# Block-sparse attention feeding a gated MLP: the four dense attention units stand first instead of last in each pair of batches

## The chip, the cores and the metric

One core of a Trainium2 chip runs the whole kernel. The metric is the device time of one execution in microseconds (us). The time before is the median of three runs, 783.1 us (782.36 to 784.8).

## The reference

Block-sparse attention over 4 batches, 8 heads, 768 positions of 64 values; a block is 32 positions, so there are 24 blocks. Its output, laid out as 3072 tokens of 512 values, goes through two matrices with a gate between them.

```python
scores = scale * np.matmul(q, k.transpose(0, 1, 3, 2))
mask = np.abs(blk_i - blk_j) <= window                                   # own block and its neighbours
mask = mask | (blk_i == 0) | (blk_j == 0) | (blk_i == n_blocks - 1) | (blk_j == n_blocks - 1)
...                                                                      # and 3 sampled blocks for each query block
attn = softmax(np.where(mask, scores, -1e9)); out = attn @ v
h = x @ w_in;  g = h * (1.0 / (1.0 + np.exp(-1.702 * h)));  return g @ w_out
```

Query blocks 0 and 23 see all 24 key blocks; every other query block sees at most eight.

## The kernel before

**Units.** Attention is cut into 48 units of 64 query positions (two blocks) with all heads. A *sparse unit* is two neighbouring blocks of 1 to 22 in one batch; it is one *item* of work. A *dense unit* is blocks 23 and 0 of one batch; it is four items (`i` picks two head pairs, `half` picks 384 of the 768 keys). A unit gives 64 columns of x for the MLP.

**An item** is: `scores` (PE; then on VectorE, DVE, the masked minimum, L283, called *least* here, and on ScalarE, ACT, the exponentials, L290), `transposes` (PE L306, then two ACT copies to `pt`, L310), `values` (PE L331 sparse, L339 dense). At the end of a unit come `factors` and `normalise` (small DVE work; for a dense unit seven small operations with a short ACT exponential between them, and three multiplies and adds, L373 and L377, instead of one), then `turn` (two PE transposes, the ACT cast `xhi`, the DVE difference `xlo`).

**Loads.** A pair of batches shares one K and one V load for each pair of blocks (`load_k`, `load_v`): contiguous pieces from SyncE's queue (SP), the sampled K blocks by SP and in the first stage also by GpSimd (POOL), the gathered V rows by POOL (L216). A dense unit has its own loads: 1.5 MB of K (L183), two V halves of 768 KB, and q. K and V have rings of two buffers each, so `loads` issues an entry when the one two before it is used up.

**The MLP** takes the tokens in 6 chunks of 512 (8 units). One chunk has 16 *ticks* (`tick`): 12 matmuls of `up`, the gate, 12 matmuls of `down`. The weights come as 64-bit words and are made into pairs of fp32r tiles during the first stage and the first 16 ticks by a generator (`weights`). For each tile it has four places where it yields: fetch and shift (L446); the low part of the tile before (L427, *last*); a DVE merge (L452) with ACT's `Abs` of the next raw tile (L422); a second DVE merge (L456) with ACT's cast (L459). It stops at the fourth `wout` tile until the first `down` is done, since `wout` has a ring of three.

**Order of the work.** Every engine works off its own list in program order. `first` runs the items of units 0 to 8 before any tick (the *first stage*), one item behind another: scores of item n, then turn of n-2, transposes of n-1, exponentials of n, values of n-1. It advances the weight generator four times per item (two before, two after), and has four spare PE transposes per item (L693). Later units are spread over the ticks by `plan`: chunk c's attention is done while the MLP works on chunk c-1. Before the change units 0 to 8 are all sparse, and dense units are 22, 23, 46 and 47.

Of the kernel before, what the change touches and what calls it, by code (L numbers as in the profile page):

```python
# [43 lines left out]
class Kernel:  # L44
# [4 lines left out]
    def __init__(self, ctx, tc, q, qd, kb, kT, v, vd, sb, w_in, w_out, out):  # L49
# [25 lines left out]
        def entry(of, **more):  # L75
            of.append({"n": len(of), "scores": 0, "values": 0, **more})
            return of[-1]
# [5 lines left out]

        for b0 in range(0, B, 2):
            for u in range(NU):
                k, v = (entry(of, b=b0, u=u) for of in (self.kent, self.vent))
                for b in (b0, b0 + 1):
                    entry(self.units, b=b, u=u)
                    item(k, v, first=True, end=True)
            for b in (b0, b0 + 1):  # L90
                entry(self.units, b=b, u=None)
                k = entry(self.kent, b=b, u=None)
                for i in range(2):
                    v = entry(self.vent, b=b, u=None, i=i)
                    for half in range(2):
                        item(k, v, i=i, half=half, first=i + half == 0, end=i + half == 2)
# [80 lines left out]
    def load_k(self, e):  # L177
# [3 lines left out]
        if u is None:  # L181
            nc.sync.dma_start(out=self.qt[r][:, 0], in_=self.qd[:, b])
            nc.sync.dma_start(out=self.kg[r].rearrange("p n b c -> p (n b c)"), in_=self.kT[b])  # L183
            self.kmidof[r] = None
            return
# [34 lines left out]
    def loads(self):  # L220

        more = True
        while more:
# [141 lines left out]
    def normalise(self, g):  # L365
# [4 lines left out]
        if not self.sparse(g):  # L370
            out.append(self.work.tile([P, 384], F32, name="ex", bufs=4)[:, 0:2 * P])
# [150 lines left out]
    def down(self, m, part):  # L522
# [13 lines left out]
        if m == NC * NF - 1:  # L536
            order = order[-1:] + order[:-1]
# [130 lines left out]
    def first(self):  # L668

        items = self.items[:CU + 1]  # L670
        assert items[CU]["unit"]["n"] == CU
# [9 lines left out]
        for n, g in enumerate(items):  # L681
# [4 lines left out]
            if n > 1:  # L686
                weights(2)
                finish(self.turn(items[n - 2]))
            if n > 0:
                finish(self.transposes(items[n - 1]))  # L690

                for _ in range(4):
                    self.nc.tensor.matmul(self.psum("a", n - 1)[0][:, 3 * P:4 * P], self.ident, self.ident, start=True, stop=True)  # L693
# [4 lines left out]
            if n > 1:  # L698
                weights(2)
        finish(self.transposes(items[CU]))  # L700
        finish(self.turn(items[CU - 1]))
# [65 lines left out]
```

## Time and profile before

| | |
|---|---|
| runs | 783.1 us median of 3 (782.36 to 784.8) |
| profiled execution: span, first to last instruction | 782.1 us |
| PE busy | 743.4 us (95%) |
| DVE busy / ACT busy | 413.0 us (53%) / 382.6 us (49%) |
| HBM read / written | 116.47 MB / 10.49 MB |

What lies around the span of the profiled execution isn't shown by itself; the median of the runs is 1.0 us above that span. The page's 40 slices show PE filled from about 80 us on and with holes before, while the DMA engines are busiest in the first 80 us. Engines named PEld, SPq and ACTq are PE's weight loads and the queues of SyncE and ScalarE.

### The profile page before, as it was taken

How to read it: one execution, taken by the hardware profiler on the slowest of the kernel's cores; microseconds unless marked ns; L12 is line 12 of the kernel's file. 1: busy time of each engine (PE TensorE's matmuls, PEld its weight loads, DVE VectorE, ACT ScalarE, POOL GpSimd, SP SyncE). 2: the span in 40 equal slices, each digit the busy share in tenths (PEclk: the TensorE clock that was granted, in tenths of full speed). 3: DMA queues.
4: the chain of work that ended last, by engine and by line, in shares of the span. 5: the costliest groups of instructions: out<-in, count | busy, mean ns of one | idle time of the engine just before them, and what ended most of it. 6: DMA issues, size and time to landing. Idle time of an engine off the chain costs nothing.

```text
span 782.1 us, 19390 instructions
## 1 busy us (share of the span) xinstructions
PE 743.4 (95%) x7648; PEld 580.5 (74%) x7648; DVE 413.0 (53%) x1076; ACT 382.6 (49%) x950; POOL 56.2 (7%) x85
## 2 busy tenths in 40 slices
PE   2876999999999999999999999999999999999997
PEld 1655787777777777787787787877778777888885
DVE  4486689978545344455445445445555444443332
ACT  1566667766555454454544544444555444333232
POOL 5222001101000001000000000000000000000000
PEclk9899999999999999999999999999999999999999
DMA  8998787886644346663544564544574231141111
GB/s 264 288 332 282 271 258 233 293 269 190 210 167 149 95 150 195 180 192 116 163 129 123 155 183 127 153 128 137 165 247 156 81 107 30 41 108 41 54 41 55
DMA packets 61117, 128.22 MB, mean 164 GB/s; under 512 B 7569, under 2 KB 26514, under 8 KB 60514
## 3 DMA queue, kind: packets, MB, share of 16 engines
q1 hardware_dynamic: 46642, 80.11, 33.8%
q0 software_dynamic: 7232, 25.51, 9.9%
q10 hardware_dynamic: 7152, 21.37, 8.2%
q8 instruction: 60, 0.98, 0.5%
q14 instruction: 31, 0.25, 0.1%
HBM read 116.47 MB, written 10.49 MB: 162 GB/s over the span
## 4 chain that ended last, share of the span: by engine, by line
PE 79%; DMA 7%; DVE 6%; ACT 4%; issue 2%; SPq 1%; ACTq 0%; DVEq 0%
PE bank L491 11%; PE bank L544 10%; PE bank L493 10%; PE bank L545 10%; PE bank L540 10%; PE bank L492 10%; PE bank L306 5%; PE bank L331 4%; PE bank L260 4%; DMA raw<-in_moe_w_in_dram 3%; PE bank L339 2%; PE bank L272 2%; DMA kg<-in_kb_dram 1%; DMA ws<-a 1%; DVE a L452 1%
## 5 line engine op out<-in xcount | busy, mean ns | idle before, releaser
L491 PE MATMUL bank<-xhi,win 128*128 128x512 f32 x384 | 158.7, 413 | 1.6 <-DVE g L506 1.3
L290 ACT ACTIVATE ex<-bank,nm 128x256 f32<-128x256 f32 (+1 forms) x208 | 99.5, 491 | 117.4 <-DVE nm L283 115.6
L506 DVE SCALAR_TENSOR_TENSOR g<-g,bank 128x512 f32<-128x512 f32 x83 | 57.1, 687 | 183.9 <-ACT g L499 183.9
L544 PE MATMUL bank<-wout,ghi 128*128 128x512 f32 x384 | 154.0, 401 | 0.0
L545 PE MATMUL bank<-wout,ghi 128*128 128x512 f32 x384 | 151.7, 395 | 0.0
L493 PE MATMUL bank<-xhi,win 128*128 128x512 f32 x384 | 151.1, 394 | 0.0
L492 PE MATMUL bank<-xlo,win 128*128 128x512 f32 x384 | 150.0, 391 | 0.0
L499 ACT ACTIVATE g<-bank 128x512 f32<-128x512 f32 x96 | 57.5, 599 | 148.3 <-PE bank L493 147.7
L540 PE MATMUL bank<-wout,glo 128*128 128x512 f32 x384 | 107.8, 394 | 0.0
L480 DVE TENSOR_TENSOR wout<-wst,wout 128x512 fp32r<-128x512 f32 x80 | 55.4, 692 | 79.6 <-ACT wout L479 78.6
L511 ACT CAST ghi<-g 128x512 fp32r<-128x512 f32 x96 | 59.7, 622 | 56.2 <-DVE g L506 56.2
L491 PEld LDWEIGHTS bank<-xhi,win 128*128 128x128 f32 x384 | 72.1, 188 | 19.7 <-DVE g L506 2.0
L540 PEld LDWEIGHTS bank<-wout,glo 128*128 128x128 f32 x384 | 72.5, 189 | 17.2
L493 PEld LDWEIGHTS bank<-xhi,win 128*128 128x128 f32 x384 | 72.1, 188 | 16.4
L545 PEld LDWEIGHTS bank<-wout,ghi 128*128 128x128 f32 x384 | 72.6, 189 | 15.6
L544 PEld LDWEIGHTS bank<-wout,ghi 128*128 128x128 f32 x384 | 72.2, 188 | 16.0
L283 DVE CUSTOM_DVE_ANT_1 bank<-bank,bias 128x256 f32<-128x256 f32 x176 | 73.8, 440 | 18.6 <-PE bank L260 15.6
L492 PEld LDWEIGHTS bank<-xlo,win 128*128 128x128 f32 x384 | 72.4, 188 | 13.0
L216 POOL DMA_INDIRECT vown<-in_v_dram,vidx x44 | 42.8, 973 | 501.5 <-PE bank L331 390.0
L310 ACT COPY pt<-bank 128x512 f32<-128x512 f32 (+1 forms) x120 | 61.1, 564 | 19.4 <-PE bank L306 19.1
L260 PE MATMUL bank<-kg,qt 64*32 64x256 f32 x1408 | 53.0, 405 | 16.2 <-DMA vmid<-in_v_dram 10.7
L519 DVE TENSOR_TENSOR glo<-g,ghi 128x512 fp32r<-128x512 f32 x96 | 65.7, 684 | 1.6 <-ACT ghi L511 1.6
(77 smaller groups left out, 815.3 us busy)
## 6 DMA issues: line engine op xcount, KB each, us to landing
wst<-ws SPq DMA_DIRECT2D x80, 256.0 KB, 2.7
kg<-in_kb_dram SPq DMA_DIRECT2D x136, 128.0 KB, 3.8
kg<-in_kb_dram SPq DMA_DIRECT2D x22, 384.0 KB, 5.1
raw<-in_moe_w_in_dram ACTq DMA_DIRECT2D x16, 512.0 KB, 5.1
raw<-in_moe_w_out_dram ACTq DMA_DIRECT2D x16, 512.0 KB, 4.6
kg<-in_kT_dram SPq DMA_DIRECT2D x4, 1536.0 KB, 7.5
vown<-in_vd_dram SPq DMA_DIRECT2D x8, 768.0 KB, 5.1
qt<-in_q_dram SPq DMA_DIRECT2D x22, 256.0 KB, 3.0
```

Source lines behind the costliest of these rows:

```text
L260: nc.tensor.matmul(sps[h][BLK * c:BLK * (c + 1), n * i:n * (i + 1)].rearrange("p (n s) -> p n s", s=BLK), self.qt[r][rows, bi, UT * pair + ...
L283: nc.vector.tensor_tensor_reduce(out=at, in0=at, in1=bias, scale=-SCALE, scalar=3.0e38, op0=ALU.add, op1=ALU.min, accum_out=un["nm"][:, ha ...
L290: nc.scalar.activation(out=ex, in_=sps[h][:, n * k:n * (k + 1)], func=AF.Exp, bias=un["nm"][:, half, c:c + 1], scale=-1.0, accum_out=un["r ...
L310: copies.append(lambda pt=pt, ps=ps, m=m: nc.scalar.copy(out=pt[:, 0:m], in_=ps[:, 0:m]))
L491: nc.tensor.matmul(h, wih[:, k], hi[:, k], start=(k == 0), stop=False)
L492: nc.tensor.matmul(h, wih[:, k], lo[:, k], start=False, stop=False)
L493: nc.tensor.matmul(h, wil[:, k], hi[:, k], start=False, stop=(k == NCT - 1))
L511: self.nc.scalar.copy(out=ghi, in_=self.g[m][0])
L519: self.nc.vector.tensor_tensor(out=glo, in0=g, in1=ghi.bitcast(F32), op=ALU.subtract)
L540: nc.tensor.matmul(o[n], glo[:, tk[n]], woh, start=False, stop=last)
L544: nc.tensor.matmul(o[n], ghi[:, tk[n]], woh, start=(f == 0), stop=False)
L545: nc.tensor.matmul(o[n], ghi[:, tk[n]], wol, start=False, stop=False)
```

## The change

The list of units begins with the four dense units (one per batch), then come the sparse ones in the order they had. Chunk 0 is now 4 dense and 4 sparse units, the other chunks are 8 sparse units each. `first` still takes units 0 to 8; these are now 21 items (16 dense, 5 sparse) instead of 9. In a dense item the generator advances once, not four times, and after a dense item there are no spare transposes. The K load of a dense unit is cut in two halves, and the first loads are K of unit 0 and both its V halves. One scratch tile of `normalise` comes from another pool, and the last `down` has its plain order again.

```diff
+        for b in range(B):
+            entry(self.units, b=b, u=None)
+            k = entry(self.kent, b=b, u=None)
+            for i in range(2):
+                v = entry(self.vent, b=b, u=None, i=i)
+                for half in range(2):
+                    item(k, v, i=i, half=half, first=i + half == 0, end=i + half == 2)
         for b0 in range(0, B, 2):
             for u in range(NU):
...
-            for b in (b0, b0 + 1):
-                entry(self.units, b=b, u=None)
...
-            nc.sync.dma_start(out=self.kg[r].rearrange("p n b c -> p (n b c)"), in_=self.kT[b])
+            kg, n = self.kg[r].rearrange("p n b c -> p (n b c)"), NPAIR // 2 * S
+            for i in range(2):
+                nc.sync.dma_start(out=kg[:, n * i:n * (i + 1)], in_=self.kT[b, :, n * i:n * (i + 1)])
...
+        if not self.knext:
+            self.load_k(self.kent[0])
+            for e in self.vent[:RING]:
+                self.load_v(e)
+            self.knext, self.vnext = 1, RING
...
-            out.append(self.work.tile([P, 384], F32, name="ex", bufs=4)[:, 0:2 * P])
+            out.append(self.work.tile([P, 4, P], F32, name="pt").rearrange("p a b -> p (a b)")[:, 0:2 * P])
...
-        if m == NC * NF - 1:
-            order = order[-1:] + order[:-1]
...
-        items = self.items[:CU + 1]
-        assert items[CU]["unit"]["n"] == CU
+        items = [g for g in self.items if g["unit"]["n"] <= CU]
...
             if n > 1:
-                weights(2)
-                finish(self.turn(items[n - 2]))
+                weights(2 if self.sparse(g) else 1)
+                if items[n - 2]["end"]:
+                    finish(self.turn(items[n - 2]))
             if n > 0:
                 finish(self.transposes(items[n - 1]))
-
+            if n > 0 and self.sparse(items[n - 1]):
+
+                spare = self.psum("a", items[n - 1]["unit"]["n"])[0][:, 3 * P:4 * P]
                 for _ in range(4):
-                    self.nc.tensor.matmul(self.psum("a", n - 1)[0][:, 3 * P:4 * P], self.ident, self.ident, start=True, stop=True)
+                    self.nc.tensor.matmul(spare, self.ident, self.ident, start=True, stop=True)
...
-            if n > 1:
+            if n > 1 and self.sparse(g):
                 weights(2)
-        finish(self.transposes(items[CU]))
-        finish(self.turn(items[CU - 1]))
+        finish(self.transposes(items[-1]))
+        finish(self.turn(items[-2]))
```

**ACT, a sparse item in the middle of the first stage.** `raw` and `a` are tiles of the weight generator, `win` and `wout` the finished weights, `ws` their copy in memory, `bank_88` and `bank_92` hold the transposes of the item before. Before:

```order
L459 CAST wout_118<-a 128x512
L414 DMA raw<-in_moe_w_in_dram 128x1024
L433 DMA ws_70<-a 128x512
L422 ACTIVATE a<-raw 128x512
L391 CAST xhi_120<-bank_91 128x4x64
L310 COPY pt<-bank_88 128x512
L310 COPY pt<-bank_92 128x512
L290 ACTIVATE ex,rs<-bank_89,nm 128x256 x2
L290 ACTIVATE ex,rs<-bank_90,nm 128x256 x2
L459 CAST win_104<-a 128x512
```

Now, at the same place (an item between two sparse items):

```order
L440 DMA ws_70<-a 128x512
L429 ACTIVATE a<-raw 128x512
L466 CAST win_104<-a 128x512
L421 DMA raw<-in_moe_w_out_dram 128x1024
L398 CAST xhi_120<-bank_87 128x4x64
L317 COPY pt<-bank_88 128x512
L317 COPY pt<-bank_92 128x512
L297 ACTIVATE ex,rs<-bank_85,nm 128x256 x2
L297 ACTIVATE ex,rs<-bank_86,nm 128x256 x2
```

The generator stands two yields further on at this place, so its cast moved from behind the exponentials to a place ahead of the copies.

**DVE, the same item.** `bank_89` and `bank_90` hold its scores (each row of the minimum is followed by a short row that reads `nm` out, left out where it only repeats). Before:

```order
L283 ISA bank_90,nm<-bank_90,bias 128x256
L283 ISA nm 128x1
L427 TENSOR_TENSOR wout_118<-a,wout_118 128x512
L452 SCALAR_TENSOR_TENSOR a<-raw,a 128x512
L392 TENSOR_TENSOR xlo_121<-bank_91,xhi_120 128x4x64
L360 TENSOR_SCALAR rg<-rs 128x4
L361 RECIPROCAL ri<-rg 128x4
L373 TENSOR_TENSOR x<-bank_87,ri 128x256
```

Now:

```order
L290 ISA bank_90,nm<-bank_90,bias 128x256
L290 ISA nm 128x1
L463 SCALAR_TENSOR_TENSOR a<-raw,a 128x512
L453 TENSOR_SCALAR a<-a 128x512
L399 TENSOR_TENSOR xlo_121<-bank_91,xhi_120 128x4x64
L367 TENSOR_SCALAR rg<-rs 128x4
L368 RECIPROCAL ri<-rg 128x4
L380 TENSOR_TENSOR x<-bank_87,ri 128x256
L434 TENSOR_TENSOR wout_119<-a,wout_119 128x512
L459 SCALAR_TENSOR_TENSOR a<-raw,a 128x512
```

The second merge and the shift now stand ahead of the division (`rg`, `ri`, `x`), and the low part and the first merge behind it.

**SP, the start.** `kg` and `qt` are the K and q buffers, `sbr` the sampled block numbers. Before:

```order
L106 DMA sbr<-in_sampled_blocks_dram 1x144
L187 DMA qt_95<-in_q_dram 128x512
L188 DMA kg_93<-in_kb_dram 128x768
L189 DMA kg_93<-in_kb_dram 128x256
L191 DMA kg_93<-in_kb_dram 128x2x256
L197 TENSOR_LOAD sbr
```

Now:

```order
L106 DMA sbr<-in_sampled_blocks_dram 1x144
L182 DMA qt_95<-in_qd_dram 128x256
L185 DMA kg_93<-in_kT_dram 128x1536 x2
L207 DMA vown_97<-in_vd_dram 128x1536
L207 DMA vown_98<-in_vd_dram 128x1536
```

The start now has no load that reads a block number first.

## Rows read from the trace of the kernel before

**Rows 1.** Windows view: length, then busy us of PE, PEld, DVE, ACT and POOL (instructions), PE's granted clock, mean DMA share, GB/s.

```profile
20.00:30.00 10.00, 7.07 (x115) 5.46 (x114) 1.51 (x7) 3.55 (x14) 0.63 (x2) 0.81 1.03 306
300.00:350.00 50.00, 49.45 (x476) 38.27 (x475) 25.66 (x71) 24.75 (x64) 3.74 (x4) 1.00 0.66 194
```

**Rows 2.** The chain of waits that ended last, first stage, to the first matmul of the MLP: start us, us, what.

```profile
19.33 13.10 DMA raw<-in_moe_w_in_dram
...
79.88 0.43 PE bank L491
```

**Rows 3.** The same chain later, the last four matmuls of `down` in a tick: from 269.06 to 277.12 a tick with a dense item, from there to 285.40 one with a dense item and a turn; from 339.37 to 353.82 two ticks with one sparse unit; from 694.72 to 700.28 a tick without attention.

```profile
269.06 0.94 PE bank L540 x4
...
277.12 0.94 PE bank L540 x4
...
285.40 0.93 PE bank L540 x4
...
339.37 0.93 PE bank L540 x4
...
353.82 0.93 PE bank L540 x4
...
694.72 0.93 PE bank L540 x4
700.28 0.93 PE bank L540 x4
```

**Rows 4.** Timeline of ACT, the gate's activation of ticks 0 and 16: start us, us, engine, line, operation.

```profile
82.91 0.60 ACT L499 ACTIVATE g<-bank 128x512 f32<-128x512 f32 x1 [0.75 <-PE bank L493]
...
201.64 0.60 ACT L499 ACTIVATE g<-bank 128x512 f32<-128x512 f32 x1 [0.65 <-PE bank L493]
```

**Rows 5.** Timeline of the start: the last operation of DVE's work on the block numbers, the first least, and PE's first transposes; then from the page's table of DMA issues the load those numbers come from (KB, us from issue to landing).

```profile
11.41 0.40 DVE L173 TENSOR_SCALAR bias<-scratch 128x88 f32<-128x88 f32 x1
16.32 0.43 DVE L283 CUSTOM_DVE_ANT_1 bank<-bank,bias 128x256 f32<-128x256 f32 x1 [4.51 <-PE bank L260]
...
19.42 0.87 PE L306 MATMUL bank<-ident,ex 128*128 128x128 f32 x3 [1.46 <-ACT ex L290]
...
scratch<-in_sampled_blocks_dram POOLq DMA_DIRECT2D x1, 72.0 KB, 5.1
```

**Rows 6.** The chain again, PE's pieces of a dense item during the ticks (scores, values, transposes).

```profile
286.33 0.81 PE bank L272 x8
287.13 0.85 PE bank L339 x24
...
290.95 0.66 PE bank L306 x6
```

**Rows 7.** Timeline of DVE and ACT, pieces of a dense item during the ticks (two copies, the first of two least, the first of two exponentials).

```profile
283.26 0.86 ACT L310 COPY pt<-bank 128x384 f32<-128x384 f32 x2
...
287.18 0.57 DVE L283 CUSTOM_DVE_ANT_0 bank<-bank,zero 128x384 f32<-128x384 f32 x1 [0.33 <-PE bank L272]
...
287.84 0.58 ACT L290 ACTIVATE ex<-bank,nm 128x384 f32<-128x384 f32 x1 [2.32 <-DVE nm L283]
```

**Rows 8.** Timeline of DVE and ACT in the first stage, four sparse items: the first least of each (with that of the item behind the last), the generator's `Abs` in three of them, and in one the division, the generator's second merge and its shift.

```profile
41.71 0.42 DVE L283 CUSTOM_DVE_ANT_1 bank<-bank,bias 128x256 f32<-128x256 f32 x1
...
44.74 0.66 ACT L422 ACTIVATE a<-raw 128x512 f32<-128x512 f32 x1 [2.63 <-DMA raw<-in_moe_w_in_dram]
...
50.18 0.43 DVE L283 CUSTOM_DVE_ANT_1 bank<-bank,bias 128x256 f32<-128x256 f32 x1 [0.55 <-PE bank L260]
...
55.25 0.42 DVE L283 CUSTOM_DVE_ANT_1 bank<-bank,bias 128x256 f32<-128x256 f32 x1
...
61.21 0.43 DVE L283 CUSTOM_DVE_ANT_1 bank<-bank,bias 128x256 f32<-128x256 f32 x1
...
63.74 0.67 ACT L422 ACTIVATE a<-raw 128x512 f32<-128x512 f32 x1 [2.12 <-DMA kg<-in_kb_dram]
...
66.64 0.42 DVE L373 TENSOR_TENSOR x<-bank,ri 128x256 f32<-128x256 f32 x1 [1.23 <-PE bank L331]
66.98 0.68 DVE L456 SCALAR_TENSOR_TENSOR a<-raw,a 128x512 int32<-128x512 int32 x1
67.58 0.42 DVE L446 TENSOR_SCALAR a<-a 128x512 int32<-128x512 int32 x1
67.92 0.42 DVE L283 CUSTOM_DVE_ANT_1 bank<-bank,bias 128x256 f32<-128x256 f32 x1
...
72.27 0.66 ACT L422 ACTIVATE a<-raw 128x512 f32<-128x512 f32 x1 [3.95 <-DMA ws<-a]
```

**Rows 9.** Windows view of PE alone, one microsecond each: length, busy us (instructions), granted clock, DMA share, GB/s.

```profile
24.00:25.00 1.00, 0.07 (x6) 1.00 1.03 268
25.00:26.00 1.00, 0.00 (x0) 1.00 1.06 313
26.00:27.00 1.00, 0.00 (x1) 0.63 1.04 287
...
63.00:64.00 1.00, 0.00 (x1) 1.00 0.97 329
64.00:65.00 1.00, 0.00 (x0) 1.00 1.04 303
65.00:66.00 1.00, 0.73 (x36) 1.00 1.00 397
```

More of the change, by code (lines that the diff above doesn't have):

```diff
@@ L89, in __init__ @@
                     item(k, v, first=True, end=True)
-            for b in (b0, b0 + 1):
-                entry(self.units, b=b, u=None)
[L92 to L96, printed above, removed]
         self.knext = self.vnext = 0
```

## The prediction

> **What bounds the kernel now.** I read the windows view first. From tick 0 on PE is the bound: between 300 and 350 us it is busy for 49.45 of 50 us at the full granted clock. Before that it isn't: between 20 and 30 us it is busy for 7.07 of 10, at a granted clock of 0.81, while the DMA engines are full (share 1.03) [rows 1]. The chain of waits says why: ACT waits 13.10 us for one raw weight tile that shares the engines with the K and V loads, and the MLP's first matmul starts only at 79.88 us [rows 2]. So the kernel is a first stage of 79.9 us in which PE has holes, and behind it a long stretch in which each PE microsecond counts. The change moves PE work between these two. It gains if the first stage grows by less than the stretch behind it shrinks.
>
> **What leaves the stretch behind.** A tick with a dense item takes 8.06 us (269.06 to 277.12), one without attention 5.56, so a dense item costs 2.50 there; the tick with a turn takes 8.28, 0.22 more [rows 3]. Sixteen items and four turns are 40.0 + 0.9 = 40.9 us. Two ticks with a sparse unit take 14.45, which is 3.33 over two plain ticks [rows 3]; the four sparse units that now come out of the first stage cost 13.3 us. **Net: -27.6 us**, all on the path, since PE has no holes there.
>
> **The first stage now: the start.** DVE works on the sampled block numbers until 11.8 (11.41 + 0.40) and its list has the first least behind that. Before, K of the first unit was late and least began at 16.32; the transposes came 3.10 us later [rows 5]. The dense K needs no block number, so I take 11.8 + 3.1 = 14.9 us for the first transposes, 4.5 earlier. Bound: the numbers' own load of 72 KB took 5.1 us [rows 5] beside smaller pieces than it has beside it now; if that costs 1 us, all shifts by 1. (The Trainium skill, "DMA: Bandwidth & Descriptors", "Queues, rings and completion order", says that each engine takes turns between queues a whole packet at a time, so a short load waits behind longer ones. No row here prices it; the 1 us is my estimate and stays in the range only.)
>
> **The dense items.** PE's pieces are 0.81 (scores), 0.85 (values) and 0.66 (transposes) [rows 6]. Values of an item need its copies (two in 0.86 on ACT [rows 7]), which need the transposes. From one item's transposes to the next it takes 0.66, half of the copies (0.43), half of the values (0.43) and the scores (0.81), with four hand-overs of some 0.05: about 2.6 us. ACT's exponentials (two of 0.58) and copies fill 2.0 of that and DVE's least 1.1 [rows 7], so both fit; so does one yield of the weight generator, except one in four. At the fourth item of a unit the cast of a weight tile stands ahead of the copies on ACT and waits for a merge of 0.68 [rows 8] that DVE has behind the least: copies 2.0 us late. In the item after it the turn waits for the division's three operations (0.34 from start to start [rows 8]) behind seven small ones: 1.5 us more, an estimate (1.0 for the three, the rest for the seven). A unit: 4 x 2.6 + 2.0 + 1.5 = **13.9 us**.
>
> The clock starts at its lower level: PE's first transposes took 0.87 us for three [rows 5], against 0.66 for six later [rows 6]. At that level PE's pieces alone are 2 x 2.32 = 4.64. I take one item at that pace, one half way (3.6) and one at 2.6; bounds are none and three, -3.0 and +3.1 us. So the transposes of the fourth item come at 14.9 + 4.6 + 3.6 + 2.6 = 25.7, those of the sixteenth, three units on, at 25.7 + 41.7 = 67.4.
>
> **The sparse items.** Before, an item that waits for nothing takes 5.07 us (50.18 to 55.25), all DVE [rows 8]. Now it can't: the generator stands two yields further on, so ACT has the cast ahead of the copies, and DVE the merge that the cast waits for behind the least. The trace has this case: in the item of 61.21 `Abs` held ACT until 63.74, 2.5 us after the least began, just where least (1.8) and merge (0.68) now end; the division then came at 66.64, 5.43 after the least [rows 8]. Behind the division there are now two operations of 0.6 each (66.98 to 67.58 is one) and 0.34 for the division: 5.43 + 0.34 + 1.2 = **7.0 us** an item. Four of them lead from 67.4 to the least of the last item at 95.4. From there to the MLP's first matmul it was 11.96 (67.92 to 79.88), of which `Abs` waited until 72.27, 1.8 longer than the 2.5 of now [rows 2, 8]: 10.1, so 105.5 us.
>
> **Clock falls.** PE now waits longer in places: by the same sums 2.2 us at a dense unit's end, 2.9 and 3.1 in the first two sparse items, 2.6 in the next three. The granted clock fell to its lower level after PE had been empty from 24.1 to 27 us, 2.9 us; it stayed up over 63 to 65.3, 2.3 us [rows 9]. So I let it fall in the first two sparse items, and hold 2.6 for a little nearer to 2.3. The price: the item of 41.71, with such a fall, took 8.47 against 6.71 for that of 61.21, and 0.5 of that was `Abs` starting later (3.03 against 2.53 after the least) [rows 8]: 1.26 a fall, **+2.5 us**. First matmul of the MLP at 108.0 instead of 79.9: **+28.1 us**.
>
> **Edits that I cost at nothing.** Dense loads: 3.1 MB for a unit and half a megabyte of weights in 13.9 us is 260 GB/s, and 397 was moved at 65 us [rows 9]; the ring lets each load go a unit ahead. If that cover fails, a late load is the second slow rival. The `pt` tile in the division: its reader, the values, is done by then; without that cover one hand-over. The last `down`'s order: within 1 us either way. The generator's lead: it stops at the fourth `wout` tile in both kernels until the first `down`, so the ticks of chunk 0 begin with nearly the same weights done. They took 118.7 us (82.91 to 201.64 [rows 4]) against 115.6 by the prices above (16 x 5.56 + 8 x 3.33); of these 3.1 us I let none go, the bounds are 0 and -3.1.
>
> **Sum.** Against the profiled execution 28.1 - 27.6 = +0.5 us on 782.1. The median of the runs is 783.1, 1.0 above that span, and I add the 0.5 to the median: **783.6 us**, no change that can be told (a measurement of this kernel tells 0.3% from none, so 780.7 to 785.5 count as the same).
>
> **Rivals.**
> *Faster: the clock holds and the lead helps.* Without any fall the sum is 783.6 - 2.5 = 781.1; if the stall of 3.1 us in chunk 0's ticks goes too, 778.0. For it: no gap that I sum in the dense items is longer than the one over which the clock held [rows 9]. Against it: the gaps of 2.9 and 3.1 us are as long as the one before which it fell, and in chunk 0's ticks DVE and ACT stay as full as they were. It wins over the forecast from 781.1 minus some 0.4 on, so it needs a part of the 3.1.
> *Slower: the clock falls at every gap.* The spare transposes that filled PE are gone in dense items. Three dense units' ends would cost 4.64 - 2.6 = 2.0 each and five sparse items 1.26 each: 12.3 on 781.1 is 793.4; half of them 787. It decides from four falls on. (The Trainium skill, "TensorE: Matmul & The Clock Gate", "HAM oscillation", tells of a kernel whose short bursts, parted by waits, each began at the low clock. By that this would be the outcome, 793.4; the trace here bears it out for the longer gaps alone [rows 9].)
> *Slower: a load is late.* A raw tile took 13.1 us when the queues were full [rows 2]. The queues fill again where the first sparse K and V meet the last dense ones; one item that waits 5 us longer gives 788.6. Against it: the cast asks for a tile fetched more than 10 us before.
> *The change doesn't do what it says:* the dense work isn't hidden in the holes at all but put behind them, since lists are worked in order. That is in the sum already: the first stage grows by as much as the rest shrinks.
>
> **How the numbers follow.** Forecast (same) 0.37. Faster 0.31: the first rival, or the start and the dense items a little shorter than I sum. Slower 0.32: 0.20 for the clock, 0.12 for a load. The range goes from 778.0, the whole first rival, to 791, most of the clock rival; the start's bounds (-3.0 to +4.1) lie inside it.
>
> **What would show it.** In the changed kernel's profile: first transposes near 15 us; 13 to 15 us from one dense unit to the next, with a hole on PE ahead of the values of its fourth item; sparse items of about 7 us with the cast ahead of the copies; the MLP's first matmul at 105 to 110; ticks 16 to 78 in an even beat of 14.45 us for two. The prediction is wrong if dense units take over 16 us (clock or loads), if sparse items go back to 5, or if the clock column shows more than three falls before the first tick.

## The result and the profile after

The changed kernel takes 788.65 us (median of 7 runs, 787.7 to 793.72) against 783.1 (7 runs, 782.2 to 786.81) of the kernel before: a ratio of 1.0075, with a 95% interval of 1.0057 to 1.0093. It is slower by three quarters of a per cent. The time lies in the predicted range, but the likeliest case, 783.6 us and no change, isn't what came; the sign is that of the slower rivals (0.32). A profile shows one execution, and executions of one kernel lie up to 8 us apart (780.63 to 788.9 in one of the runs below), so medians decide between kernels, and a profile tells only where its own execution's time went.

The profiled execution has a span of 786.1 us, 4.0 more than before (it is the shortest of its seven; by the medians the loss is 5.55). Where they come from is read in two places. First the chain of waits that ended last, start us, us, what; its last row answers to [rows 2]. The first five are a regular dense item, those from 90.94 on a sparse one; both are read further below.

```profile
37.10 0.49 PE bank L313 x3
...
37.66 0.49 ACT pt L317
...
38.20 0.95 PE bank L346 x24
39.15 0.81 PE bank L279 x8
39.95 0.49 PE bank L313 x3
...
90.94 0.55 DVE a L463
91.58 0.34 ACTq L421
...
92.31 1.08 ACT pt L317 x2
93.44 0.95 PE bank L338 x48
94.41 0.42 DVE x L380
94.83 0.60 DVE win L434
95.43 0.60 DVE a L459
...
111.80 0.43 PE bank L498
```

The MLP's first matmul comes at 111.80 us instead of 79.88: the first stage is **31.9 us longer**. Next the timeline of ACT: a wait for a raw weight tile, the cast at the end of three dense units and in the first sparse item, then the gate's activation of ticks 0, 16 and 80 (the first two answer to [rows 4]).

```profile
20.62 0.66 ACT L429 ACTIVATE a<-raw 128x512 f32<-128x512 f32 x1 [3.66 <-DMA raw<-in_moe_w_in_dram]
...
30.08 0.62 ACT L466 CAST win<-a 128x512 fp32r<-128x512 f32 x1 [2.17 <-DVE a L463]
...
44.69 0.62 ACT L466 CAST win<-a 128x512 fp32r<-128x512 f32 x1 [2.17 <-DVE a L463]
...
61.41 0.62 ACT L466 CAST wout<-a 128x512 fp32r<-128x512 f32 x1 [2.17 <-DVE a L463]
...
77.14 0.62 ACT L466 CAST win<-a 128x512 fp32r<-128x512 f32 x1 [3.29 <-DVE a L463]
...
114.80 0.60 ACT L506 ACTIVATE g<-bank 128x512 f32<-128x512 f32 x1 [0.87 <-PE bank L500]
...
232.47 0.60 ACT L506 ACTIVATE g<-bank 128x512 f32<-128x512 f32 x1 [0.93 <-PE bank L500]
...
691.48 0.60 ACT L506 ACTIVATE g<-bank 128x512 f32<-128x512 f32 x1 [3.06 <-PE bank L500]
```

From tick 0 to tick 80 it is 576.7 us, where it was 604.5 (82.91 to the same tick at 687.40). The stretch behind the first stage is **27.8 us shorter**, and from tick 80 to the last, tick 95, both take 83.3. 31.9 - 27.8 = 4.1, the whole difference of the spans but 0.1. So the question is only why the first stage grew by 31.9 and not by 28.1.

The timeline of DVE gives its parts: the first least of the first dense item, and of the five sparse items.

```profile
12.81 0.57 DVE L290 CUSTOM_DVE_ANT_0 bank<-bank,zero 128x384 f32<-128x384 f32 x1
...
74.64 0.43 DVE L290 CUSTOM_DVE_ANT_1 bank<-bank,bias 128x256 f32<-128x256 f32 x1 [1.50 <-PE bank L267]
...
82.13 0.42 DVE L290 CUSTOM_DVE_ANT_1 bank<-bank,bias 128x256 f32<-128x256 f32 x1
...
95.95 0.43 DVE L290 CUSTOM_DVE_ANT_1 bank<-bank,bias 128x256 f32<-128x256 f32 x1
...
102.85 0.43 DVE L290 CUSTOM_DVE_ANT_1 bank<-bank,bias 128x256 f32<-128x256 f32 x1
```

The dense part ends at 74.64 (forecast 67.4). The first sparse item takes 7.49 us, the next two 13.82, the fourth 6.90 (forecast 7.0 each). From the last least to the first matmul it is 8.95 (forecast 10.1, and 2.5 more for clock falls). The dense part is late by 7.2, the rest early by 3.4.

The windows view of the changed kernel (length, then busy us of PE, PEld, DVE, ACT and POOL with instructions, PE's clock, DMA share, GB/s) shows a second thing that matters below:

```profile
20.00:60.00 40.00, 30.55 (x383) 19.96 (x384) 20.38 (x69) 24.32 (x70) 1.68 (x3) 0.83 0.68 236
60.00:110.00 50.00, 33.69 (x688) 24.89 (x693) 33.56 (x116) 30.76 (x94) 12.87 (x17) 0.97 0.94 308
0.00:110.00 110.00, 70.72 (x1128) 48.06 (x1136) 61.50 (x224) 59.64 (x175) 17.70 (x43) 0.92 0.83 280
```

The DMA engines have room in the dense part (share 0.68) and next to none behind it (0.94). In the first 110 us 30.8 MB are moved (280 GB/s times 110 us); before, the first 80 us moved 23.3 (291 GB/s).

### The profile page after: what moved, and what is told of

Same layout as the page of the kernel before. It is cut to its first block, busy times and chain, and to the rows that moved or that the text cites. A ratio compares the mean times of both kernels' runs of the same rounds, so it can differ in the third digit from the quotient of the medians.

```text
span 786.1 us, 19362 instructions
## 1 busy us (share of the span) xinstructions
PE 738.0 (94%) x7616; PEld 576.3 (73%) x7616; DVE 411.8 (52%) x1076; ACT 385.4 (49%) x950; POOL 53.3 (7%) x79
## 4 chain that ended last, share of the span: by engine, by line
PE 78%; DVE 9%; ACT 5%; DMA 4%; issue 2%; ACTq 1%; SPq 0%; DVEq 0%; POOLq 0%
PE bank L498 11%; PE bank L545 10%; PE bank L500 10%; PE bank L550 10%; PE bank L549 10%; PE bank L499 10%; PE bank L338 5%; PE bank L267 5%; PE bank L313 4%; DVE bank L290 2%; PE bank L346 2%; ACT pt L317 2%; DVE a L463 1%; PE bank L279 1%; DVE a L459 1%
## 5 line engine op out<-in xcount | busy, mean ns | idle before, releaser
L317 ACT COPY pt<-bank 128x512 f32<-128x512 f32 (+1 forms) x120 | 61.4, 561 | 26.3 <-PE bank L313 25.6
L313 PEld LDWEIGHTS bank<-ident,ex 128*128 128x128 f32 x448 | 52.5, 144 | 18.2 <-ACT ex L297 7.2
```

The costliest lines, as they stand in the source:

```text
L313: nc.tensor.transpose(ps[:, m], g["ex"][h, i][:, k * P:(k + 1) * P], self.ident)
L317: copies.append(lambda pt=pt, ps=ps, m=m: nc.scalar.copy(out=pt[:, 0:m], in_=ps[:, 0:m]))
```

## The experiments

The theory to begin with: the loss is made by lists that are worked in order, that is by the cast of a weight tile ahead of the copies, by the raw tile that comes late, and by clock falls in the holes that these leave. The rivals: the loads (the dense ones and those behind them), the clock by itself, and the small edits. "First matmul" is the MLP's first; "chunk 0" is from the gate's activation of tick 0 to that of tick 16; ratios are to the kernel before. First matmul, chunk 0 and span are those of the one profiled execution, whose time, where it is on record, is 1.6 to 1.7 us over its span; the median is that of all executions.

| run | first matmul, us | chunk 0, us | span, us | median, us | ratio [95%] |
|---|---|---|---|---|---|
| before | 79.9 | 118.7 | 782.1 | 783.1 | |
| changed | 111.8 | 117.7 | 786.1 | 788.65 | 1.0075 [1.0057, 1.0093] |
| raw tiles early | 113.1 | 119.0 | 788.0 | 789.82 | 1.0085 [1.0064, 1.0105] |
| cast moved in sparse items | 110.8 | 118.4 | 785.2 | 787.48 | 1.006 [1.0038, 1.0082] |
| cast moved in dense items | 111.4 | 117.6 | 785.0 | 784.5 | 1.0014 [0.9995, 1.0033] |
| spare transposes in dense items | 116.4 | 118.5 | 791.0 | 793.9 | 1.0149 [1.012, 1.0178] |
| before, generator later | 81.8 | 120.0 | 784.9 | 784.53 | 1.0016 [0.9993, 1.0038] |
| two yields in sparse items | 108.6 | 118.9 | 783.5 | 785.31 | 1.0017 [0.9999, 1.0036] |
| more loads in sparse items | 120.7 | 117.3 | 793.9 | 795.99 | 1.0151 [1.0115, 1.0186] |
| dense cast moved, two yields | 97.3 | 119.2 | 772.5 | 778.62 | 0.9943 [0.9924, 0.9962] |
| dense cast moved, no yields | 98.0 | 122.5 | 776.3 | 780.39 | 0.9979 [0.9959, 1.0] |
| small edits undone | 113.3 | 118.8 | 788.4 | 790.01 | 1.0077 [1.005, 1.0104] |
| sparse pair between dense units | 95.9 | 120.0 | 771.4 | 775.39 | 0.9899 [0.9868, 0.993] |
| before, two yields | 69.9 | 124.1 | 777.1 | 779.95 | 0.9975 [0.9957, 0.9992] |

**Raw tiles early.** The first advance of the generator stands ahead of the first loads.

```diff
+        next(self.conv)
         self.loads()
         self.first()
...
-            if n == 1:
-                next(self.conv)
```

> The changed kernel, but the first two raw weight tiles are fetched ahead of all loads instead of behind the first item. Theory (lists): ACT's first Abs waits 3.7 us for its raw tile and holds the copies behind it, and the clock falls in that hole; here the wait and the first fall go, so the MLP's first matmul comes 3 to 4 us earlier than 111.8 and the time is about 785. Rival (bytes): the 1 MB of raw tiles now stands beside K of unit 0, which lands some 3 us later (1 MB at about 300 GB/s); what is won at Abs is lost at the first scores, and the first matmul stays within 1 us of 111.8.

The wait and the first clock fall went, and the first sparse least came 3.35 us earlier, at 71.29. Yet the first matmul came 1.3 us later than in the changed kernel. That is nearer to the rival, but not for its reason: K came in time, the first least stood at 13.15, and the time was lost in the sparse items. PE's granted clock is lower there too than in the changed kernel (a mean of 0.85 from 63 to 110 us instead of 0.96). In the chain there (start us, us, what) stands a new kind of wait:

```profile
67.69 7.52 DMA qt<-in_q_dram
75.22 0.33 ACTq L421
75.66 0.49 ACT pt L317
```

The copies wait for ACT's fetch of a weight tile ahead of them, and the fetch waits until a load of q, of SP's queue and with nothing in common, has landed. In the built program the transfers of SP and ACT use eight completion counters (semaphores that a transfer raises when it has landed) in turn, and this fetch carries a wait for the transfer that had its counter before, the load of q.

**Cast moved in the sparse items**, by two more yields behind the item ahead of the last dense one.

```diff
-            if n > 1 and self.sparse(g):
+            if n > 1 and (self.sparse(g) or self.sparse(items[n + 1])):
                 weights(2)
```

> The changed kernel, but with two more yields of the weight generator behind the item ahead of the last dense one, so that in the sparse items the cast stands behind the exponentials, as it did before. Theory (lists): the five sparse items of 6.9 to 7.5 us take 5.1 to 5.6, the MLP's first matmul comes at 104 to 106, the time is about 782. Rival (loads): the sparse items wait for the sparse K and V behind the dense ones; they stay over 6.3 us and the first matmul over 109.

The sparse items were 6.77, 6.48, 13.17 and 4.75 us. The theory's 5.1 to 5.6 came once, below even that, and one item took 13; the first matmul moved by 1.0. Of the rival, the bounds for the first matmul held, but not its reason: it isn't K or V that the long item waits for. The first row is of the chain (start us, us, what), the second of ACT's timeline:

```profile
81.35 11.08 DMA ws<-a
```

```profile
92.51 0.66 ACT L429 ACTIVATE a<-raw 128x512 f32<-128x512 f32 x1 [6.12 <-DMA ws<-a]
```

ACT's `Abs`, still ahead of the copies, waits 6.12 us for the save of the weight tile whose buffer it is to write. The save took 11.08 us to land, and its issue had waited for a K load. So the list held this item too, through a late transfer. The median, 787.48, can't be told from that of the changed kernel.

**Cast moved in the dense items**, the yield behind the values instead of ahead of the transposes.

```diff
-                weights(2 if self.sparse(g) else 1)
+                weights(2 if self.sparse(g) else 0)
...
-            if n > 1 and self.sparse(g):
-                weights(2)
+            if n > 1:
+                weights(2 if self.sparse(g) else 1)
```

> The changed kernel, but in a dense item the one yield of the generator stands behind the values instead of ahead of the transposes, so at a dense unit's end the cast no longer stands ahead of the copies of the fourth item. Theory (lists): from one dense unit's end to the next 12.6 to 13 us instead of 14.6 to 16.7; the first matmul at 104 to 107. Rival (division): the fourth item's values and the turn wait for the small DVE operations, and the cast's wait was beside that; the units stay within 0.7 us of what they were and the first matmul over 109.

The dense units took 13.56 and 13.52 us (first least at 28.51, 42.07 and 55.59), and the first sparse least came at 66.13, 8.5 us earlier. So the list had held them, though for 1.1 us a unit rather than 2. More came from the start: 5.3 of the 8.5 us lie ahead of the fifth item (first least at 28.51, in the changed kernel at 33.81), since the yield's new place takes the wait for the first raw tile off the copies' way too, and with it the first clock fall. In this profile the first matmul came only 0.4 us earlier: 8.1 of 8.5 us were lost again in the sparse items (8.27, 11.27, 8.48, 7.94). The chain says by what in the item of 11.27:

```profile
68.51 11.78 DMA vmid<-in_v_dram
80.37 0.33 ACTq L421
...
81.02 0.60 ACT pt L317
81.66 2.03 PE bank L338 x64
```

Again ACT's fetch stands ahead of the copies and waits for another queue's load, here V. That item is 4.4 us longer than in the changed kernel, about half of what was lost. In the rest the clock has a part. PE alone in a window over the sparse items (length, busy us with instructions, granted clock, DMA share, GB/s), this run and then the changed kernel:

```profile
63.00:110.00 47.00, 31.41 (x588) 0.78 0.82 261
63.00:110.00 47.00, 32.81 (x674) 0.96 0.95 309
```

The clock is at its lower level from 69 to 76, from 79 to 86 and from 96 to 103 us, where the changed kernel has one fall of 3.4 us, while the DMA engines are less full than there; where PE is at the lower level, its values take 2.03 us (the chain above) instead of 1.41 in the changed kernel. How the rest divides isn't shown. And by its median the edit isn't lost: 784.5 us, a ratio of 1.0014 against 1.0075 with intervals that don't touch, so it takes back most of the 0.75%. The profiled execution (786.69 us) had the lowest mean granted clock of its ten, 0.985 where the others had 0.989 to 0.993. With the 673.6 us that this profile has behind the first matmul, an execution at the median would have it near 109 (an estimate), still later than expected. The theory is right for the dense part and in part for the stage.

**Spare transposes in the dense items**, four each, in a bank that the next scores overwrite.

```diff
+            elif n > 0:
+                spare = self.psum("s", g["n"] + 1)[0][:, 0:P]
+                for _ in range(4):
+                    self.nc.tensor.matmul(spare, self.ident, self.ident, start=True, stop=True)
```

> The changed kernel with four spare PE transposes in each dense item too, in a bank that the next scores overwrite. Rival (clock): the holes without them let the clock fall three times; with them the falls go or become shorter and the first matmul comes 2 to 4 us earlier than 111.8, the time is 785 to 786. Theory (lists): the holes are waits for ACT and DVE and stay as long; spares of 0.9 us can't fill a hole of 3.7, so at most one fall goes, and the first matmul stays within 1.3 us of 111.8; up to 1 us is lost where no hole was.

PE alone in a window over the dense part (length, busy us with instructions, granted clock, DMA share, GB/s), then DVE's first least of two dense items that are a unit apart:

```profile
20.00:70.00 50.00, 42.82 (x575) 1.00 0.76 259
```

```profile
48.28 0.56 DVE L290 CUSTOM_DVE_ANT_0 bank<-bank,zero 128x384 f32<-128x384 f32 x1
...
64.38 0.56 DVE L290 CUSTOM_DVE_ANT_0 bank<-bank,zero 128x384 f32<-128x384 f32 x1
```

The clock stays at its upper level through these 50 us, and a dense unit takes 16.10 us where 14.61 was the undisturbed one before: the spares stand in PE's list between the transposes and the values, and cost 1.5 us a unit. The first matmul came 4.6 us later. So holding the clock up in this way costs more than it gives, and the theory had the sign but not the size. What the falls themselves cost isn't parted from the spares' own time: in the changed kernel the unit with a fall took 2.1 us more than the one without. The sparse items had spares all along, and there the clock still fell twice (80 to 83 and 104 to 107 us). The clock as a part of the loss isn't refuted.

**Before, with the generator later.** Two yields are left out at the first place in the kernel before.

```diff
-                weights(2)
+                weights(2 if n > 2 else 0)
                 finish(self.turn(items[n - 2]))
```

> The kernel before, but the weight generator starts two yields later, so that in its nine sparse items the cast and the merge that it waits for stand ahead of the copies, as in the changed kernel. Theory (lists): the items from 41.7 to 67.9, 6.55 us each in the mean, take 6.9 to 7.0; the MLP's first matmul comes 2 to 4 us later than 79.9. Rival (loads): those items already wait for K, raw tiles and the save of weights, and the cast's place costs nothing beside that; the first matmul stays within 1 us of 79.9.

DVE's first least of three items:

```profile
57.79 0.42 DVE L283 CUSTOM_DVE_ANT_1 bank<-bank,bias 128x256 f32<-128x256 f32 x1
...
64.71 0.43 DVE L283 CUSTOM_DVE_ANT_1 bank<-bank,bias 128x256 f32<-128x256 f32 x1
...
71.61 0.43 DVE L283 CUSTOM_DVE_ANT_1 bank<-bank,bias 128x256 f32<-128x256 f32 x1
```

6.92 and 6.90 us from one to the next: the beat of the changed kernel's sparse items, made in the kernel before by the place of the cast alone. The first matmul came 1.9 us later, a little under what was expected, since the items there were at 6.55 by their loads already. The time is unclear within 0.3%.

**Two yields in the sparse items**, both behind the exponentials.

```diff
-                weights(2 if self.sparse(g) else 1)
+                weights(0 if self.sparse(g) else 1)
```

> The changed kernel with two yields of the generator in a sparse item instead of four, both behind the exponentials: the cast is out of the copies' way, and only one raw tile of 512 KB is fetched in two items. Theory now (two bounds, one just below the other: the lists, and the bytes of raw tiles, saves, K and V): with both lowered the sparse items take 5.1 to 5.8 us and the first matmul comes at 104 to 107, the time is 781 to 784 if chunk 0's ticks still get their weights in time. Rival (K and V alone are the bound): the items stay over 6.3 us as with the cast moved alone, the first matmul over 109.

5.64, 11.08, 4.99 and 4.43 us: three items as expected, one of 11, and the first matmul 3.2 us earlier, outside both forecasts. The chain of the long item:

```profile
74.63 12.02 DMA kg<-in_kb_dram
...
87.00 2.21 PE bank L267 x32
```

That is K of the second sparse pair. Its buffer comes free with the last scores of the last dense unit (two buffers), and then it and the V behind it queue with what is under way.

**The same with the dense cast moved**, and then **with no yield at all** in the sparse items. The diff is that of the first; in the second `weights(1)` stands there for dense items alone.

```diff
-                weights(2 if self.sparse(g) else 1)
...
-            if n > 1 and self.sparse(g):
-                weights(2)
+            if n > 1:
+                weights(2 if self.sparse(g) else 1)
```

> The changed kernel with the dense items' yield behind the values and two yields in a sparse item, behind the exponentials. Theory (two bounds): the dense units take 13.5 us and the sparse items 5.1 to 6; the first matmul at 99 to 102 and the time 776 to 779, below both kernels. Rival (K and V loads are the bound): what the dense items win is lost in the sparse items, the first matmul stays over 107 and the time over 782.

> The same with no yield at all in the sparse items, so that nothing of the weights is fetched or made there. Theory (two bounds): the sparse items take 4.5 to 5.3 us, the first matmul comes at 97 to 100; chunk 0's ticks have 20 yields more to do than in the changed kernel and take 118 to 124 us (117.7 there), so the time is 775 to 783. Rival (K and V loads are the bound): sparse items over 6.3 us in spite of it.

With two yields the sparse items are 5.61, 7.95, 6.37 and 4.43 us, and the first matmul comes at 97.3, 14.5 us earlier than in the changed kernel: a bit faster than expected there. Each edit alone gave 0.4 and 3.2 in its profile. By the medians it looks otherwise: from the changed kernel's ratio the one edit takes 0.61 points, the other 0.58, and both take 1.32, about their sum; the execution that was profiled with both is the shortest of its six (774.15, median 778.62). With no yields it comes at 98.0 and chunk 0 takes 3.3 us more. One item still takes 11.73 us, and PE's timeline has its wait, at a time when no transfer of weights is under way:

```profile
79.23 2.22 PE L267 MATMUL bank<-kg,qt 64*32 64x256 f32 x32 [6.09 <-DMA vmid<-in_v_dram]
```

The scores read K and q alone; the last K piece of the second sparse pair was issued at 67.21, took 11.7 us to land and came ahead of the V load that the row names. So what waits is the loads of the second sparse pair themselves.

**More loads in the sparse items**: SP loads 512 KB that nobody reads, behind the loads of each.

```diff
+            if self.sparse(g):
+                for k in range(2):
+                    more = self.work.tile([P, DM], F32, name="wst")
+                    self.nc.sync.dma_start(out=more, in_=self.v[1][0:P, DM * k:DM * (k + 1)])
```

> The changed kernel with 512 KB more loaded by SyncE behind the loads of each sparse item of the first stage, into tiles that nobody reads. Theory (two bounds, the loads just below the lists): the sparse items, 6.9 to 7.5 us with full DMA engines, go to 8 or more (512 KB at some 320 GB/s is 1.6 us), and the first matmul comes 5 to 9 us later than 111.8. Rival (lists alone): there is room beside the lists, the first matmul moves by less than 2 us.

The first matmul came 8.9 us later; the sparse items took 7.48, 11.67, 8.03 and 6.90. So the changed kernel has no room for more loads there. The extra time came mostly in two places, the item of 11.67 and the way from the last least to the first matmul (12.6 instead of 8.95), not 1.6 in each item, so it is waiting for landings more than the bytes' own time. The chain has K loads of 8.85, 10.73 and 9.70 us there, and the last two end at ACT's save of a weight tile, ahead of the copies, not at PE's scores. The extra transfers also use up completion counters; the run doesn't part the two.

**Small edits undone**: the dense K in one load, the last `down` in its old order.

```diff
-            kg, n = self.kg[r].rearrange("p n b c -> p (n b c)"), NPAIR // 2 * S
-            for i in range(2):
-                nc.sync.dma_start(out=kg[:, n * i:n * (i + 1)], in_=self.kT[b, :, n * i:n * (i + 1)])
+            nc.sync.dma_start(out=self.kg[r].rearrange("p n b c -> p (n b c)"), in_=self.kT[b])
...
+        if m == NC * NF - 1:
+            order = order[-1:] + order[:-1]
```

> The changed kernel with two of its small edits undone: the dense K comes in one load again instead of two halves, and the last down has its old order. Theory: neither lies on the path; the time stays within 0.3% of the changed kernel's (786.3 to 791). Rival (the small edits cost): one of them made part of the 0.75%, and the time falls under 786.

Within 0.2% of the changed kernel: they cost nothing that can be told. The scratch tile's pool wasn't tried.

**The first sparse pair between the second and the third dense unit**, beside the dense cast moved and two yields.

```diff
+        dense(0)
+        dense(1)
+        pair(0, 0)
+        dense(2)
+        dense(3)
```

> The kernel with the dense yield behind the values and two yields in a sparse item, and besides with the first sparse pair of units between the second and the third dense unit instead of behind the fourth. Theory (the wait of 7 to 12 us for K and V of the second sparse pair comes from the border, where 3 MB of sparse loads meet the last dense ones in two buffers): the sparse loads are spread over the dense work, the first matmul comes 2 to 4 us earlier than at 97 us, and the time is 774 to 777. Rival (all bytes of the first stage at the rate of the engines are the bound): the first matmul stays within 1 us of 97, the time at 778 to 779.

DVE's first least of the five sparse items:

```profile
38.46 0.43 DVE L300 CUSTOM_DVE_ANT_1 bank<-bank,bias 128x256 f32<-128x256 f32 x1 [1.56 <-PE bank L277]
...
44.03 0.43 DVE L300 CUSTOM_DVE_ANT_1 bank<-bank,bias 128x256 f32<-128x256 f32 x1
...
75.95 0.43 DVE L300 CUSTOM_DVE_ANT_1 bank<-bank,bias 128x256 f32<-128x256 f32 x1 [1.51 <-PE bank L277]
...
81.56 0.43 DVE L300 CUSTOM_DVE_ANT_1 bank<-bank,bias 128x256 f32<-128x256 f32 x1
...
87.32 0.43 DVE L300 CUSTOM_DVE_ANT_1 bank<-bank,bias 128x256 f32<-128x256 f32 x1 [1.49 <-PE bank L277]
```

5.57, 5.61 and 5.76 us from one to the next within a group: no long item is left. The windows view now has the engines fuller in the dense part:

```profile
20.00:60.00 40.00, 33.25 (x603) 23.20 (x606) 27.75 (x98) 30.22 (x92) 4.66 (x7) 1.00 0.95 329
```

One clock fall, of 3.4 us, is left in the first stage. The time fits the theory, 775.39 us and a ratio of 0.9899, below both kernels; to the run with the dense units ahead (0.9943) it is 3.2 us, with intervals that overlap by a little. The first matmul gained 1.4 us, between the two forecasts: with a share of 0.95 (0.98 from 60 to 95 us) the bytes are now nearly the bound that the rival named.

**Before, with two yields.** Is it the order of the units that gains, or only the yields?

```diff
-            if n > 1:
-                weights(2)
-                finish(self.turn(items[n - 2]))
+            if n > 1:
+                finish(self.turn(items[n - 2]))
```

> The kernel before with two yields of the generator in a sparse item instead of four, behind the exponentials: the same relief, without the new order of the units. Theory (the first stage of before is bound by its loads, and dense work is what can lie beside them): 3 to 4 MB of weights fewer in the first stage let the first matmul come at 70 to 75 us instead of 79.9, but chunk 0's ticks get 14 yields more and take 3 to 5 us longer; the time is 778 to 782, so that of the 0.990 of the last kernel 3 us or more belong to the order of the units. Rival (the order gives nothing): the time is 774 to 777, as low as with the dense units ahead.

As the theory had it: the first matmul 10 us earlier, chunk 0 5.4 us longer (a little over the bound), and 779.95 us. The yields alone take 0.25% from the kernel before; the kernel with the dense units ahead, relieved in both places, stands 0.57% under it, and 1.0% with the sparse pair between them. Of these two only the last has an interval that doesn't touch that of the yields alone, so the gain of a new order is shown for the mixed one.

## Why the prediction came out as it did

The stretch behind came as forecast, and so did the mechanism of the sparse items. The first stage came 3.8 us longer than forecast, with larger errors inside that partly cancel, so that the range held is in part luck. Of the signs of being wrong that the prediction named one came: a dense unit of over 16 us. The first matmul, at 111.80, lies outside its 105 to 110.

**The stretch behind: right.** -27.8 against -27.6: 26.7 of it from tick 16 to tick 80, which took 459.0 us (232.47 to 691.48) where it was 485.8, and 1.1 in chunk 0's ticks, inside the bounds of 0 and -3.1. The tail didn't move.

**The start: right within its bounds.** The first least stood at 12.81 instead of 11.8, since the block numbers' load came 1.5 us later (DVE's first operation on them at 8.00, before at 6.54); the 1 us of the range was for that. The turns between queues that the Trainium skill tells of ("DMA: Bandwidth & Descriptors", "Queues, rings and completion order") agree with the delay, but no run here isolates them. Transposes came at 14.29 (forecast 14.9).

**The first items: a term that was missing, and one too many.** The transposes of the fourth item came at 28.13, not 25.7. The forecast gave 3.0 us to a start at the lower clock; from the first transposes to the second it took 2.89 us (14.29 to 17.18) instead of 4.6. It let nothing wait for the first raw tile; that is fetched behind the first exponentials, takes 6.6 us, and holds ACT's `Abs` for 3.66 and the copies behind it. The kernel before has the same wait, as ACT's timeline there shows:

```profile
30.03 0.67 ACT L422 ACTIVATE a<-raw 128x512 f32<-128x512 f32 x1 [6.19 <-DMA raw<-in_moe_w_in_dram]
```

The 13.10 us of [rows 2], which the prediction takes for ACT's wait, are the second raw tile's time from issue to landing; ACT stood idle 6.19 us for the first tile and 1.75 for the second. PE's windows of the changed kernel (length, busy us, clock, DMA share, GB/s) show what follows from the hole, and two more falls:

```profile
20.00:21.00 1.00, 0.00 (x0) 0.50 0.32 131
...
26.00:27.00 1.00, 1.00 (x19) 0.61 1.01 350
...
47.00:48.00 1.00, 0.59 (x8) 0.63 1.02 422
...
78.00:79.00 1.00, 0.81 (x15) 0.50 1.00 335
```

The clock was back by 27, 55 and 82 us.

**The dense units: mis-sized.** 13.9 was forecast; from cast to cast it was 14.61, 16.72 and 15.73. A regular item takes 2.86, not 2.6. The chain of the changed kernel has the term, from 37.10 to 39.95: three transposes 0.49, a copy 0.49, the values 0.95, the scores 0.81. The forecast counted half of the values (0.43). But PE's next scores stand behind all of them, and only the other half of the transposes and copies overlaps. The unit of 16.72 has one clock fall (47 to 54), 2.1 us above the undisturbed 14.61; the last has the first sparse item's longer wait (3.29 for the merge).

**The sparse items: right, by the mechanism named.** 6.9 after the first, and the chain (from 90.94) runs as forecast: second merge, ACT's fetch and copies, values, division, low part, first merge, and then the next least. The kernel before shows the same beat once its cast stands there.

**Clock falls: three instead of two**, and one of them where it was put: that of 78 lies in the first sparse item, none of the other four has one, and two came in the dense part, where the forecast had none. Its ground was weak: the 0.63 of the window from 26 to 27 us in [rows 9] puts the fall near 26.3 (an estimate), some 2.2 us after PE ran empty, and over 2.3 us from 63 on the clock stayed up, so the length of a hole alone didn't tell. The clock rival (a fall at every gap) didn't come. But the two falls are part of the 7.2 us, and the spares, which cost 1.5 us a unit themselves, don't tell what the kernel would be without them.

**The cover that was thin: loads at no cost.** To the forecast's 28.1 the parts add up to 31.9 as they stand: dense part +7.2, sparse items +0.2, last item -1.15, falls -2.5. What that doesn't tell is that the terms aren't free to move. In the profiles, of a dense part 8.5 us shorter 0.4 was left at the first matmul, of the cast out of the sparse items' way 1.0, and without the wait for the raw tile it came later. Late transfers took a good part of the rest, and the clock was lower there: from 63 to 110 us its mean was 0.78, 0.85 and 0.85 in these three, 0.96 in the changed kernel. The medians don't show this for the dense cast, whose edit takes back 0.61 of the 0.75 points. The forecast checked the bytes of the dense units alone (260 GB/s) and stopped there. At the border the second sparse pair can't be loaded before the last dense scores, and with two yields or none the item that waits for it took 7.95 to 11.73 us, the others 4.3 to 6.4. That is the second slow rival's place. In the changed kernel only a raw tile (3.66) was late in plain sight; that the border's loads lie hidden behind the lists there is argued from these runs, not shown.

**What stays open.** How the loss of 4 us in the changed kernel divides between lists, late transfers and clock falls isn't settled: the dense cast's new place takes a wait for a transfer and a clock fall along, and the two yields take away list work and transfers at once. No run changes the clock alone. How much of a late load is bytes, and how much the completion counters that SP and ACT share, wasn't parted.

## What to carry to other kernels

Before moving work into a stage with idle engines, sum the bytes of that whole stage, not of the moved part: here a stage at 0.89 of its DMA engines took 7.5 MB more. When one fix shows nothing in a profile, look at the median of many executions first, then in the trace for a second wait or a clock fall that took its place, and try it beside other fixes before dropping it. An optional background load at the head of an in-order list holds everything behind it twice over, by its own landing and by the earlier transfer that it must wait for; fewer of them in the full stage and a mixed order of heavy and light loads gained 1.0% where the moved work alone lost 0.75%.

## What the runs showed of the hardware that was not expected

Fetches on ACT had to wait for loads of another queue that took 7.5 and 11.8 us to land, through the completion counter that both use in turn. PE holes of the same 2.12 us (ahead of the values at 31.1, 45.7 and 62.5) had no fall, a fall at 47, and none; one of 2.34 (ahead of 86.05) had none. A 128 KB piece of K took 12.02 us to land while the engines were at a share near 1.0. A dense part without a clock fall was followed by three in the sparse items, a mean of 0.78 over 47 us, and 50 us with the clock at its upper level, held by spares, came with a slower kernel.
